# VectorE makes a block product's residual one step later in a three-layer kernel bound by TensorE

## The chip, the cores and the metric

The kernel runs on one core of one Trainium2 chip. The metric is the device time of one execution in microseconds (us), lower is better. The core's engines are TensorE (PE; its weight loads are shown apart, as PEld), VectorE (DVE), ScalarE (ACT), GpSimd (POOL) and SyncE (SP, which issues the DMAs). They run side by side, each in its own order, and wait for one another by semaphores.

## The reference

Three layers follow each other; all numbers are float32.

```
# 1 attention: 2 batches, 8 heads, 768 tokens, head size 64; 8 global columns, a window of 96
a = softmax(scale * q @ k.T + bias, where kept);  x = (a @ v) as [1536, 512]
# 2 a dense mixture of 4 experts: w1 [4, 512, 1024], w2 [4, 1024, 512]
for e in range(4):
    h = np.maximum(x @ w1[e], 0.0)
    out += p[:, e:e + 1] * (h @ w2[e])
# 3 one more layer: 512 -> 1024, h * softmax(h), normalised, 1024 -> 512
```

The change concerns `np.maximum(x @ w1[e], 0.0)` in layer 2.

## The kernel before

A float32 matrix is held as a high part and a residual (value less high part), both in TensorE's `float32r` format, and a product is the sum of three matmuls: high by high, high by residual, residual by high. So each hidden value h is needed twice: as high part `hh`, which ScalarE writes as the relu of a PSUM bank, and as residual `hl`, which VectorE makes from the same bank and `hh`.

Layer 2 runs over eight half experts (`he` 0 to 7, half of w1's columns each). The 1536 tokens are three blocks of 512. From `he` 1 on, the first product x @ w1 of two blocks together is made by a scheme of Strassen's kind with seven block products in place of eight (`paired_groups`, lines 646 to 698). From `he` 2 on, the third block is done in the same way in two halves of 256 tokens (`tail_groups`, lines 567 to 608). Seven passes of the first and six of the second run in all, one pass of each in each `he`: first the tail, then its second product h @ w2 (four groups of twelve matmuls, `g2`, line 523), then the paired products, then eight groups `g2`.

In `paired_groups` the products come in the order 1, 2, 6, 5, 7, 4, 3, each for q = 0 and q = 1 in turn (below "7q0" is product 7 for q = 0). A product is six matmuls of 512 columns (line 676). The products of one q share three PSUM banks: 1, 6, 7 and 4 add up in bank a, 2 in bank b, 5 and 3 in bank c. After each product stands what reads it:

- After 1, 6 and 5 ScalarE copies the bank to SBUF (`kept`, line 681).
- After 2, 7 and 3 VectorE adds a kept copy and a bank into bank b or c ("the sum", line 684); then `hidden` (line 658) lets ScalarE write `hh` (the relu, line 662) and VectorE write `hl` ("the residual", line 663).
- After 4 there is no sum: `hidden` reads bank a itself.

`tail_groups` does the same for one q with twelve matmuls of 256 columns to a product (line 596), in the order 1, 2, 6, 5, 7, 3, 4; its copy, sum, relu and residual are lines 601, 606, 582 and 583.

Each engine works its instructions off in the order in which this code issues them; nothing reorders them. So the residual of a product stands on VectorE's queue directly behind its sum, and waits there for ScalarE's relu. Between the products `st.tick` (line 414) issues other work: weights are loaded and split on ScalarE and GpSimd, and pieces of the third layer's weights are converted from 64 bits with up to four VectorE instructions at a time (lines 186 to 203).

What waits for what around the change:

```
684  nc.vector.tensor_tensor(out=t, in0=kept[...], in1=ps, op=ALU.add)                # the sum
662  nc.scalar.activation(th, src, AF.Relu)                                           # hh
663  nc.vector.scalar_tensor_tensor(out=tl, in0=src, ..., in1=th, max, subtract)      # hl
529  if given and c0 == 2 * HALF and dt == 0:
530      terms.sort(key=lambda x: (x[2] is hl, x[0] % 2))
```

Product 4 adds on in bank a, which the sum after 7 reads, so 4q1 can start only when the sum after 7q1 is done. After a tail pass the first group `g2` takes all `hh` terms first and the `hl` terms last (line 530); its first matmul needs the relus after 2 and 3, since each of its operands holds columns of both.

Of the kernel before, what the change touches and what calls it, by code (L numbers as in the profile page):

```python
# [8 lines left out]
F32 = mybir.dt.float32  # L9
# [5 lines left out]
AF = mybir.ActivationFunctionType  # L15
ALU = mybir.AluOpType
# [35 lines left out]
def kernel(ctx, tc, ep, qk, vp, nn, pr, wall, w64, gl, out):  # L52
    nc = tc.nc
# [57 lines left out]
    with tc.manual_schedule():  # L111
# [27 lines left out]
        def iota(cols, step, base, cm):  # L139
# [23 lines left out]
                                       op0=ALU.is_le, op1=ALU.mult)  # L163
        nc.vector.scalar_tensor_tensor(out=fi, in0=ng, scalar=float(NG_MAX), in1=flg[:, 1:2],
                                       op0=ALU.is_le, op1=ALU.mult)
# [41 lines left out]
    def stream(arm):  # L207
# [148 lines left out]
        def refresh(he):  # L356

            def due(k, *ops):
                for f in ops:
                    st.due.setdefault(st.now + k, []).append(f)  # L360

            (load0, sums0, (r0, r1, s0, s1)), (load2, sums2, (r2, r3, s2, s3)) = (
                first_weights(8 * he + q) for q in (0, 2))
            load0()
            yield
            load2()
            if he == 1:
                due(2, r0[0], r1[0])
                due(3, r0[1], r1[1])
                due(4, r2[0], r3[0])  # L370
                due(5, r2[1], r3[1])
                due(7, sums0)
                due(8, s0[0], s1[0])
                due(9, s0[1], s1[1])
                due(10, sums2)
                due(12, s2[0], s3[0])
                due(13, s2[1], s3[1])
                return
            r0[0]()
            r1[0]()  # L380
            due(1, r0[1], r1[1], r2[0], r3[0])
            due(2, sums0)
            due(3, r2[1], r3[1], s0[0], s1[0])
            due(4, s0[1], s1[1])
            due(5, sums2)
            due(6, s2[0], s3[0])
            due(7, s2[1], s3[1])
# [88 lines left out]
        def two_tiles():  # L476
            return [st.hp.tile([128, 2, HALF], F32R, tag=tag, name=f"{arm}{tag}") for tag in ("hh", "hl")]
# [83 lines left out]
        def left(he, q, i):  # L561
            n = 8 * he + 2 * q
            w, k0 = {1: (st.pieces[n], 0), 2: (st.pieces[n], 2), 4: (st.pieces[n + 1], 2), 6: (st.pieces["S", n], 0),
                     3: (st.pieces["S", n], 2), 7: (st.pieces["S", n + 1], 0), 5: (st.pieces["S", n + 1], 2)}[i]
            return w.rearrange("p w (k f) -> p w k f", k=4)[:, :, k0:k0 + 2]

        def tail_groups(he, h3):

            q_ = HALF // 2
            lo, hi = slice(2 * HALF, 2 * HALF + q_), slice(2 * HALF + q_, 3 * HALF)  # L570
            right = {i: [[x[:, k0 + j, cols] for j in range(2)] for x in (xh, xl)]
                     for i, k0, cols in ((1, 0, lo), (2, 2, lo), (3, 2, hi), (4, 0, hi))}
            for i, f in ((5, 0), (6, 1), (7, 2)):
                right[i] = [[st.xt3[f][j][:, b] for j in range(2)] for b in range(2)]
            twos = [two_tiles() for _ in range(2)]
            for d, w in zip(h3, range(2)):
                d[:] = [twos[odd][w].rearrange("p h (q c) -> p q h c", q=2)[:, q] for q in range(2) for odd in range(2)]
            banks, kept = {}, {}

            def hidden(src, odd, half):  # L580
                th, tl = (x[:, half] for x in twos[odd])
                nc.scalar.activation(th, src, AF.Relu)  # L582
                nc.vector.scalar_tensor_tensor(out=tl, in0=src, scalar=0.0, in1=th.bitcast(F32),
                                               op0=ALU.max, op1=ALU.subtract)

            for i in (1, 2, 6, 5, 7, 3, 4):
                c = {1: "a", 6: "a", 7: "a", 4: "a", 2: "b", 5: "c", 3: "c"}[i]
                opens = i in (1, 2, 5)
                if opens:
                    banks[c] = st.psp.tile([128, 512], F32, tag="g", name=f"{arm}g")  # L590
                ps, x = banks[c], right[i]
                for q in range(2):
                    w = left(he, q, i)
                    for j in range(2):
                        for m, (a, b) in enumerate(((0, 0), (0, 1), (1, 0))):
                            nc.tensor.matmul(ps[:, q_ * q:q_ * q + q_], lhsT=w[:, a, j], rhs=x[b][j],  # L596
                                             start=(opens and q == j == m == 0), stop=(j == 1 and m == 2),
                                             skip_group_check=True)
                if i in (1, 6, 5):
                    kept[i] = sc_b[2 if i == 6 else 0]  # L600
                    nc.scalar.copy(kept[i], ps)
                elif i == 4:
                    hidden(ps, 1, 0)
                else:
                    t = banks["c" if i == 3 else "b"]
                    nc.vector.tensor_tensor(out=t, in0=kept[{2: 1, 7: 5, 3: 6}[i]], in1=ps, op=ALU.add)  # L606
                    hidden(t, i == 7, i != 2)
                yield i
# [37 lines left out]
        def paired_groups(he, h1, h2):  # L646

            lo, hi = slice(0, HALF), slice(HALF, 2 * HALF)

            def raw_x(k0, cols):  # L650
                return [[x[:, k0 + j, cols] for j in range(2)] for x in (xh, xl)]

            right = {1: raw_x(0, lo), 2: raw_x(2, lo), 3: raw_x(2, hi), 4: raw_x(0, hi)}
            for i, f in ((5, 0), (6, 1), (7, 2)):
                right[i] = [[xt[:, f, b, j] for j in range(2)] for b in range(2)]
            banks, kept, twos = {}, {}, []

            def hidden(src, dst, ft):
                if ft < 2:
                    twos[:] = two_tiles()  # L660
                th, tl = (x[:, ft // 2] for x in twos)
                nc.scalar.activation(th, src, AF.Relu)  # L662
                nc.vector.scalar_tensor_tensor(out=tl, in0=src, scalar=0.0, in1=th.bitcast(F32),  # L663
                                               op0=ALU.max, op1=ALU.subtract)
                dst[0][ft], dst[1][ft] = th, tl

            def product(q, i):
                c = {1: "a", 6: "a", 7: "a", 4: "a", 2: "b", 5: "c", 3: "c"}[i]
                if i in (1, 2, 5):
                    pool = st.ps1 if (q, i) == (1, 5) else st.psp  # L670
                    banks[q, c] = pool.tile([128, 512], F32, tag="g", name=f"{arm}g")
                ps = banks[q, c]
                w, x = left(he, q, i), right[i]
                for j in range(2):
                    for m, (a, b) in enumerate(((0, 0), (0, 1), (1, 0))):
                        nc.tensor.matmul(ps, lhsT=w[:, a, j], rhs=x[b][j],  # L676
                                         start=(i in (1, 2, 5) and j == 0 and m == 0), stop=(j == 1 and m == 2),
                                         skip_group_check=(i not in (1, 2, 5)))
                if i in (1, 6, 5):
                    kept[q, i] = sc_b[(2 if i == 6 else 0) + q]  # L680
                    nc.scalar.copy(kept[q, i], ps)
                if i in (2, 7, 3):
                    t = banks[q, "c" if i == 3 else "b"]
                    nc.vector.tensor_tensor(out=t, in0=kept[q, {2: 1, 7: 5, 3: 6}[i]], in1=ps, op=ALU.add)  # L684
                    hidden(t, *((h1, 2 * q) if i == 2 else (h2, 2 * q + 1) if i == 7 else (h2, 2 * q)))
                elif i == 4:
                    hidden(ps, h1, 2 * q + 1)

            for i in (1, 2, 6, 5, 7, 4, 3):
                for q in range(2):  # L690
                    product(q, i)
                if i == 4:
                    weights = refresh(he + 1) if he < NHE - 1 else iter(())
                    next(weights, None)
                yield i
            next(weights, None)
            if he == NHE - 1:
                st.second += range(14)
# [226 lines left out]

    def fast_arm():
        st = stream("f")
        with ExitStack() as es:
            enter = es.enter_context
# [418 lines left out]

    def general_arm():
        st = stream("g")  # L1350
        for _ in st.load_p():
            pass
# [170 lines left out]
```

## Time and profile before

| | |
|---|---|
| median of 3 runs | 740.16 us (740.01 to 740.42) |
| the profiled execution's own time | 740.11 us |
| its span, first to last instruction | 738.2 us |
| granted TensorE clock, mean | 0.999 |
| PE busy | 725.0 us (98%), 3917 matmuls |
| PEld busy | 601.8 us (82%) |
| DVE busy | 473.0 us (64%) |
| ACT busy | 293.2 us (40%) |
| POOL busy | 260.7 us (35%) |

A matmul's row in the trace lasts longer than the step from its start to the next one's, because matmuls are pipelined; a row with x6 merges six of them. A row of the windows gives a stretch, its length, the busy time of PE, PEld, DVE, ACT and POOL (with the number of instructions), the granted clock, the DMA engines' busy share and GB/s. "Idle before" in square brackets is the time in which the engine did nothing ahead of the row, and what ended it.

### The profile page before, as it was taken

The numbers are of one execution on the slowest core, as the hardware profiler recorded it, in microseconds if no ns is written. First come the engines' busy times: TensorE is split into PE (matmuls) and PEld (weight loads), VectorE is DVE, ScalarE is ACT, GpSimd is POOL, SyncE is SP. The second block draws the span as 40 slices with busy tenths as digits, with TensorE's granted clock in tenths as the row PEclk, the third lists the DMA queues.
The fourth block names the chain that finished last, engine by engine and source line by source line (L and its number), as shares of the span: only waits on it lengthen the run. The fifth ranks groups of instructions, "written<-read, shape, count | busy, mean of one in ns | idle before, by whom it ended". The sixth has DMA issues, their size and how long they took to land.

```text
span 738.2 us, 11012 instructions
## 1 busy us (share of the span) xinstructions
PE 725.0 (98%) x3917; PEld 601.8 (82%) x3917; DVE 473.0 (64%) x1040; ACT 293.2 (40%) x668; POOL 260.7 (35%) x294
## 2 busy tenths in 40 slices
PE   8999999999999999999999999999999999999997
PEld 6688877888888888888888888888888888888886
DVE  6787868647694686568568567766843546655551
ACT  4777766432532334133243334323333223243252
POOL 5600044475683164208306424630744231000000
PEclk9999999999999999999999999999999999999999
DMA  8633421212242232223222222322100910222221
GB/s 252 169 94 100 113 84 44 86 43 72 73 135 91 60 101 85 72 87 108 78 72 85 86 72 94 107 72 82 48 28 29 366 62 12 60 77 75 64 73 49
DMA packets 49984, 65.69 MB, mean 89 GB/s; under 512 B 6656, under 2 KB 31488, under 8 KB 49920
## 3 DMA queue, kind: packets, MB, share of 16 engines
q1 hardware_dynamic: 49360, 64.47, 28.0%
q8 instruction: 33, 0.54, 0.3%
q10 hardware_dynamic: 560, 0.43, 0.2%
q14 instruction: 31, 0.25, 0.1%
HBM read 49.12 MB, written 11.56 MB: 82 GB/s over the span
## 4 chain that ended last, share of the span: by engine, by line
PE 85%; DVE 5%; ACT 4%; issue 3%; POOL 2%; DMA 0%; DVEq 0%; ACTq 0%; POOLq 0%
PE fg L532 35%; PE fg L676 14%; PE fo L904 9%; PE fh L843 9%; PE fg L596 6%; PE fg L503 4%; PE x L1102 2%; PE sps L998 2%; PE pt L1080 2%; DVE fg L684 1%; DVE fg L606 1%; ACT fhh L582 1%; PE wp L1185 1%; ACT fhh L662 1%; DVE fhl L663 1%
## 5 line engine op out<-in xcount | busy, mean ns | idle before, releaser
L532 PE MATMUL fg<-fhh,wV 128*128 128x512 f32 (+1 forms) x800 | 243.5, 384 | 3.4 <-ACT fhh L582 3.3
L532 PEld LDWEIGHTS fg<-fhh,wV 128*128 128x128 f32 x800 | 148.3, 188 | 36.7 <-ACT fhh L582 4.5
L532 PE MATMUL fg<-fhl,wV 128*128 128x512 f32 (+1 forms) x400 | 149.3, 381 | 0.0
L532 PEld LDWEIGHTS fg<-fhl,wV 128*128 128x128 f32 x400 | 75.0, 188 | 14.7 <-DVE fhl L518 0.2
L303 POOL TENSOR_TENSOR wR<-kr,wR 128x512 fp32r<-128x512 f32 (+1 forms) x28 | 29.0, 1061 | 111.5 <-ACT wR L295 71.5
L663 DVE SCALAR_TENSOR_TENSOR fhl<-fg,fhh 128x512 fp32r<-128x512 f32 x56 | 38.1, 690 | 31.8 <-ACT fhh L662 31.8
L676 PE MATMUL fg<-xt,fwS 128*128 128x512 f32 x252 | 58.3, 389 | 0.0
L676 PE MATMUL fg<-xh,wR 128*128 128x512 f32 x168 | 56.0, 394 | 0.7
L662 ACT ACTIVATE fhh<-fg 128x512 fp32r<-128x512 f32 x56 | 32.7, 598 | 58.9 <-DVE fg L684 55.1
L676 PEld LDWEIGHTS fg<-xt,fwS 128*128 128x128 f32 x252 | 47.3, 188 | 9.8
L545 POOL TENSOR_TENSOR scr<-scr,kr 128x512 f32<-128x512 f32 x24 | 31.0, 1291 | 63.1 <-DVE kr L544 63.1
L904 PE MATMUL fo<-xt,ft 128*128 128x512 f32 (+1 forms) x234 | 51.8, 374 | 0.0
L540 DVE TENSOR_TENSOR fg<-fg,pb 128x512 f32<-128x512 f32 x60 | 41.6, 693 | 14.5 <-PE fg L532 14.4
L904 PEld LDWEIGHTS fo<-xt,ft 128*128 128x128 f32 x234 | 41.5, 188 | 7.6
L1058 ACT ACTIVATE p<-p,mn 128x256 f32<-128x256 f32 x68 | 33.8, 498 | 27.5 <-DVE mn L1053 27.5
L893 POOL TENSOR_SCALAR fva<-fva 128x1 f32<-128x1 f32 x12 | 3.2, 265 | 114.2 <-ACT scr L892 114.2
L541 DVE TENSOR_TENSOR scr<-fg,scr 128x512 f32<-128x512 f32 x60 | 41.5, 692 | 2.0
L684 DVE TENSOR_TENSOR fg<-kr,fg 128x512 f32<-128x512 f32 x42 | 28.9, 689 | 21.6 <-PE fg L676 18.8
L676 PEld LDWEIGHTS fg<-xh,wR 128*128 128x128 f32 x168 | 31.5, 188 | 10.0 <-DVE fg L684 3.6
L503 PE MATMUL fg<-xh,wR 128*128 128x512 f32 (+1 forms) x128 | 39.5, 373 | 0.0
L544 DVE TENSOR_TENSOR kr<-fg,pb 128x512 f32<-128x512 f32 x24 | 16.6, 692 | 31.4 <-PE fg L532 27.9
L200 ACT CAST fr<-fcvs 128x256 fp32r<-128x256 f32 x32 | 11.9, 373 | 61.1 <-DVE fcvs L196 48.4
(206 smaller groups left out, 1468.3 us busy)
## 6 DMA issues: line engine op xcount, KB each, us to landing
kr<-in_wall_dram SPq DMA_DIRECT2D x42, 256.0 KB, 2.7
fr<-in_w_dram SPq DMA_DIRECT2D x32, 256.0 KB, 2.6
w_dram<-fr SPq DMA_DIRECT2D x32, 256.0 KB, 2.4
v<-in_vp_dram SPq DMA_DIRECT2D x10, 512.0 KB, 3.5
frawt<-in_wall_dram SPq DMA_DIRECT2D x14, 256.0 KB, 2.7
xt<-w_dram SPq DMA_DIRECT2D x6, 512.0 KB, 9.9
kr<-in_qk_dram SPq DMA_DIRECT2D x22, 128.0 KB, 3.8
out_dram<-scr SPq DMA_DIRECT2D x11, 256.0 KB, 2.2
```

The source lines that it names most:

```text
L503: nc.tensor.matmul(ps[:, :n], lhsT=w[:, a, k], rhs=b[:, k, cols], start=(k == 0 and i == 0), stop=(k == 3 and i == 2))
L532: nc.tensor.matmul(ps[:, :n], lhsT=w[:, a, k], rhs=b[k], start=(i == 0), stop=(i == 11))
L540: nc.vector.tensor_tensor(out=ps[:, :n], in0=ps[:, :n], in1=pb[:, cols], op=ALU.mult)
L541: nc.vector.tensor_tensor(out=a, in0=ps[:, :n], in1=a, op=ALU.add)
L596: nc.tensor.matmul(ps[:, q_ * q:q_ * q + q_], lhsT=w[:, a, j], rhs=x[b][j], start=(opens and q == j == m == 0), stop=(j == 1 and m == 2), ...
L662: nc.scalar.activation(th, src, AF.Relu)
L663: nc.vector.scalar_tensor_tensor(out=tl, in0=src, scalar=0.0, in1=th.bitcast(F32), op0=ALU.max, op1=ALU.subtract)
L676: nc.tensor.matmul(ps, lhsT=w[:, a, j], rhs=x[b][j], start=(i in (1, 2, 5) and j == 0 and m == 0), stop=(j == 1 and m == 2), skip_group_ch ...
L684: nc.vector.tensor_tensor(out=t, in0=kept[q, {2: 1, 7: 5, 3: 6}[i]], in1=ps, op=ALU.add)
L843: nc.tensor.matmul(ps[:, hf], lhsT=a[:, k, cs], rhs=w[:, b], start=(k == 0 and i == 0), stop=(k == 3 and i == 2))
L904: nc.tensor.matmul(ps, lhsT=a[:, fc % 4], rhs=wo[fc][:, b, c0:c0 + n], start=(fc == 0 and i == 0), stop=(fc == 7 and i == 2))
L1058: nc.scalar.activation(p[:, a], p[:, a], AF.Exp, bias=mn[:, a:a + 1], scale=-1.0, accum_out=st_rs[u][:, a, 0:1])
```

## The change

A helper `rectified` keeps a list of residuals that have not been issued yet. It first issues those on the list, then the relu of the new product, and then puts the new product's residual on the list. Since the sum of a product is issued before `hidden` is called, the order on VectorE becomes: sum of this product, residual of the product before. The list is also emptied after a copy to `kept`, after product 4 in the tail and after product 3q1 in the paired products.

```
+        def rectified(residuals, src, th, tl):
+            while residuals:
+                residuals.pop(0)()
+            nc.scalar.activation(th, src, AF.Relu)
+            residuals.append(lambda: nc.vector.scalar_tensor_tensor(
+                out=tl, in0=src, scalar=0.0, in1=th.bitcast(F32), op0=ALU.max, op1=ALU.subtract))
...
             def hidden(src, odd, half):
                 th, tl = (x[:, half] for x in twos[odd])
-                nc.scalar.activation(th, src, AF.Relu)
-                nc.vector.scalar_tensor_tensor(out=tl, in0=src, scalar=0.0, in1=th.bitcast(F32),
-                                               op0=ALU.max, op1=ALU.subtract)
+                rectified(residuals, src, th, tl)
...
                     nc.scalar.copy(kept[i], ps)
+                    while residuals:
+                        residuals.pop(0)()
                 elif i == 4:
                     hidden(ps, 1, 0)
+                    residuals.pop(0)()
...
             def hidden(src, dst, ft):
                 if ft < 2:
                     twos[:] = two_tiles()
                 th, tl = (x[:, ft // 2] for x in twos)
-                nc.scalar.activation(th, src, AF.Relu)
-                nc.vector.scalar_tensor_tensor(out=tl, in0=src, scalar=0.0, in1=th.bitcast(F32),
-                                               op0=ALU.max, op1=ALU.subtract)
+                rectified(residuals, src, th, tl)
...
                     nc.scalar.copy(kept[q, i], ps)
+                    while residuals:
+                        residuals.pop(0)()
...
+                if i == 3:
+                    residuals.pop(0)()
                 yield i
```

VectorE's order in the paired products of `he` 4, from the sum after 7q0 on. Before (lines 684 and 663 are sum and residual; the number behind `fg` is the bank that is read; 193 to 198 are a conversion of weights):

```order
L684 TENSOR_TENSOR fg_3790<-kr_78,fg_3768 128x512
L663 SCALAR_TENSOR_TENSOR fhl_3857<-fg_3790,fhh_3856 128x512
L684 TENSOR_TENSOR fg_3802<-kr_78,fg_3776 128x512
L663 SCALAR_TENSOR_TENSOR fhl_3857<-fg_3802,fhh_3856 128x512
L663 SCALAR_TENSOR_TENSOR fhl_3876<-fg_3768,fhh_3875 128x512
L663 SCALAR_TENSOR_TENSOR fhl_3876<-fg_3776,fhh_3875 128x512
L193 TENSOR_SCALAR fcvs_1830<-fr64_3767 128x256
L194 SCALAR_TENSOR_TENSOR fcvs_1830<-fr64_3767,fcvs_1830 128x256
L198 TENSOR_TENSOR fr64_3767<-fr64_3767,fcvs_1830 128x256
L684 TENSOR_TENSOR fg_3827<-kr_78,fg_3827 128x512
L663 SCALAR_TENSOR_TENSOR fhl_3903<-fg_3827,fhh_3902 128x512
L684 TENSOR_TENSOR fg_3835<-kr_78,fg_3835 128x512
```

The same place with the change (sum is now line 692, residual line 571):

```order
L692 TENSOR_TENSOR fg_3790<-kr_78,fg_3768 128x512
L692 TENSOR_TENSOR fg_3801<-kr_78,fg_3776 128x512
L571 SCALAR_TENSOR_TENSOR fhl_3857<-fg_3790,fhh_3856 128x512
L571 SCALAR_TENSOR_TENSOR fhl_3857<-fg_3801,fhh_3856 128x512
L571 SCALAR_TENSOR_TENSOR fhl_3875<-fg_3768,fhh_3874 128x512
L193 TENSOR_SCALAR fcvs_1830<-fr64_3767 128x256
L194 SCALAR_TENSOR_TENSOR fcvs_1830<-fr64_3767,fcvs_1830 128x256
L198 TENSOR_TENSOR fr64_3767<-fr64_3767,fcvs_1830 128x256
L692 TENSOR_TENSOR fg_3827<-kr_78,fg_3827 128x512
L571 SCALAR_TENSOR_TENSOR fhl_3875<-fg_3776,fhh_3874 128x512
L692 TENSOR_TENSOR fg_3835<-kr_78,fg_3835 128x512
```

The sum after 7q1 has moved ahead of the residual of 7q0, and the residual of 4q1 has moved behind the conversion and the sum after 3q0.

VectorE's order in the tail pass of `he` 4, from the sum after 2 to the last residual. Before (sum line 606, residual line 583):

```order
L606 TENSOR_TENSOR fg_3595<-kr_78,fg_3595 128x512
L583 SCALAR_TENSOR_TENSOR fhl_3578<-fg_3595,fhh_3577 128x512
L606 TENSOR_TENSOR fg_3595<-kr_78,fg_3581 128x512
L583 SCALAR_TENSOR_TENSOR fhl_3580<-fg_3595,fhh_3579 128x512
L606 TENSOR_TENSOR fg_3626<-kr_78,fg_3626 128x512
L583 SCALAR_TENSOR_TENSOR fhl_3578<-fg_3626,fhh_3577 128x512
L583 SCALAR_TENSOR_TENSOR fhl_3580<-fg_3581,fhh_3579 128x512
```

With the change (sum line 614, residual line 571):

```order
L614 TENSOR_TENSOR fg_3595<-kr_78,fg_3595 128x512
L571 SCALAR_TENSOR_TENSOR fhl_3578<-fg_3595,fhh_3577 128x512
L614 TENSOR_TENSOR fg_3595<-kr_78,fg_3581 128x512
L614 TENSOR_TENSOR fg_3626<-kr_78,fg_3626 128x512
L571 SCALAR_TENSOR_TENSOR fhl_3580<-fg_3595,fhh_3579 128x512
L571 SCALAR_TENSOR_TENSOR fhl_3578<-fg_3626,fhh_3577 128x512
L571 SCALAR_TENSOR_TENSOR fhl_3580<-fg_3581,fhh_3579 128x512
```

Here the sum after 3 has moved ahead of the residual of 7; the rest stands as it stood. On PE, ACT, POOL and SP no instruction moves.

## Rows read from the trace of the kernel before

**Rows 1.** The page: busy time, share of the span, instructions.
```profile
PE 725.0 (98%) x3917; PEld 601.8 (82%) x3917; DVE 473.0 (64%) x1040; ACT 293.2 (40%) x668; POOL 260.7 (35%) x294
```

**Rows 2.** Waits: who waited for whom, us in total, times, longest.
```profile
PEld fg L676 <- DVE fg L684: 3.6, 7, 0.5
...
PE fg L532 <- ACT fhh L582: 3.3, 6, 0.6
```

**Rows 3.** The chain that ended last, 329 to 430 us: start, us, what.
```profile
346.58 7.21 PE fg L596 x60
...
387.86 21.76 PE fg L532 x96
```

**Rows 4.** Windows: one pass of a half expert, `he` 4: us, busy by engine.
```profile
368.42:431.45 63.03, 62.38 (x314) 52.85 (x313) 44.57 (x85) 22.15 (x43) 25.22 (x24) 1.00 0.26 81
```

**Rows 5.** Timeline of DVE and ACT, paired products of `he` 4, 380 to 388 us.
```profile
380.77 0.70 DVE L684 TENSOR_TENSOR fg<-kr,fg 128x512 f32<-128x512 f32 x1 [1.98 <-PE fg L676]
381.50 0.60 ACT L662 ACTIVATE fhh<-fg 128x512 fp32r<-128x512 f32 x1 [1.57 <-DVE fg L684]
382.13 0.69 DVE L663 SCALAR_TENSOR_TENSOR fhl<-fg,fhh 128x512 fp32r<-128x512 f32 x1 [0.66 <-ACT fhh L662]
382.74 0.69 DVE L684 TENSOR_TENSOR fg<-kr,fg 128x512 f32<-128x512 f32 x1
386.41 0.42 DVE L193 TENSOR_SCALAR fcvs<-fr 128x256 int32<-128x256 int32 x1
```

**Rows 6.** Timeline of PE and PEld, same place, 381 to 390 us.
```profile
381.86 0.39 PE L676 MATMUL fg<-xh,wR 128*128 128x512 f32 x1
382.77 0.19 PEld L676 LDWEIGHTS fg<-xh,wR 128*128 128x128 f32 x1
382.99 0.98 PE L676 MATMUL fg<-xh,wR 128*128 128x512 f32 x2
383.48 0.19 PEld L676 LDWEIGHTS fg<-xh,wR 128*128 128x128 f32 x1 [0.52 <-DVE fg L684]
383.81 0.39 PE L676 MATMUL fg<-xl,wR 128*128 128x512 f32 x1
387.69 0.39 PE L532 MATMUL fg<-fhh,wV 128*128 128x512 f32 x1
389.96 0.39 PE L532 MATMUL fg<-fhl,wV 128*128 128x512 f32 x1
```

**Rows 7.** Timeline of the tail pass of `he` 4, 353 to 360 us.
```profile
353.61 0.28 PE L596 MATMUL fg<-xh,fwS 128*128 128x256 f32 x1
353.87 0.70 DVE L606 TENSOR_TENSOR fg<-kr,fg 128x512 f32<-128x512 f32 x1 [2.22 <-PE fg L596]
355.05 0.28 PE L596 MATMUL fg<-xh,wR 128*128 128x256 f32 x1
355.23 0.69 DVE L583 SCALAR_TENSOR_TENSOR fhl<-fg,fhh 128x512 fp32r<-128x512 f32 x1 [0.66 <-ACT fhh L582]
355.84 0.69 DVE L606 TENSOR_TENSOR fg<-kr,fg 128x512 f32<-128x512 f32 x1
356.37 0.28 PE L596 MATMUL fg<-xh,wR 128*128 128x256 f32 x1
356.56 1.09 ACT L582 ACTIVATE fhh<-fg 128x512 fp32r<-128x512 f32 x2 [1.36 <-DVE fg L606]
357.20 2.14 PE L532 MATMUL fg<-fhh,wV 128*128 128x512 f32 x8 [0.55 <-ACT fhh L582]
359.18 1.08 PE L532 MATMUL fg<-fhl,wV 128*128 128x512 f32 x4
```

**Rows 8.** Groups by line: busy, mean ns, idle before: PE's rows of line 676.
```profile
L676 PE MATMUL fg<-xh,wR 128*128 128x512 f32 x168 | 56.0, 394 | 0.7
```

**Rows 9.** DVE's wait in a conversion; the load of a piece (KB, us to landing).
```profile
DVE fr L203 <- ACT fr L200: 3.0, 5, 1.0
...
fr<-in_w_dram SPq DMA_DIRECT2D x32, 256.0 KB, 2.6
```

More of the change, by code (lines that the diff above doesn't have):

```diff
@@ L577, in tail_groups @@
                 d[:] = [twos[odd][w].rearrange("p h (q c) -> p q h c", q=2)[:, q] for q in range(2) for odd in range(2)]
-            banks, kept = {}, {}
+            banks, kept, residuals = {}, {}, []
             def hidden(src, odd, half):
                 th, tl = (x[:, half] for x in twos[odd])
-                nc.scalar.activation(th, src, AF.Relu)
-                nc.vector.scalar_tensor_tensor(out=tl, in0=src, scalar=0.0, in1=th.bitcast(F32),
-                                               op0=ALU.max, op1=ALU.subtract)
+                rectified(residuals, src, th, tl)
             for i in (1, 2, 6, 5, 7, 3, 4):
@@ L655, in paired_groups @@
                 right[i] = [[xt[:, f, b, j] for j in range(2)] for b in range(2)]
-            banks, kept, twos = {}, {}, []
+            banks, kept, twos, residuals = {}, {}, [], []
             def hidden(src, dst, ft):
```

## The prediction

> **What bounds the kernel now.** The page's busy time first: PE is busy for 725.0 of 738.2 us, the next engine, DVE, for 473.0 [rows 1]. So only time in which TensorE stands still can be won, some 13 us by this count, and the reader should look for what stops it. The view of the waits names what the change can touch [rows 2]: 7 weight loads of the paired products waited 0.5 us each for the sum (line 684), and 6 first matmuls of `g2` after a tail pass waited 0.6 us each for a relu (line 582). 7 and 6 are the numbers of paired and of tail passes, so it is the same place each time, and I work out one pass, `he` 4.
>
> Pace without a stall: 96 matmuls of 512 columns in 21.76 us, 0.227 us a step, and 60 of 256 columns in 7.21 us, 0.120 us [rows 3]. A pass has 228 of the first and 84 of the second, which makes 51.7 + 10.1 = 61.8 us; it lasts 63.03 [rows 4]. TensorE thus loses 1.2 us in a pass. The timelines show where.
>
> *Paired products.* Product 4q0 starts at 381.86; its last weights are loaded at 382.77 for a matmul at 382.99 [rows 6]. One step later, 383.00, those of 4q1 would be loaded, for a matmul at 383.22. They are loaded at 383.48, after 0.52 us of waiting, and the matmul behind the first starts at 383.81 where 383.45 was due: 0.36 us late. By the first matmul of `g2`, 19 steps after 382.99, it is 387.69 for 387.30, 0.39 late. The load waited for the sum after 7q1 (382.74 to 383.43), and that sum, on VectorE's queue, for the residual of 7q0 at 382.13, which in turn stood 0.66 us idle until the relu of 7q0 (from 381.50) was there [rows 5].
>
> *Tail.* The last matmul of product 4 starts at 356.37; `g2` was due at 356.49. Its first relu runs from 356.56, and the load and matmul start at 357.20. The ninth matmul starts at 359.18, due at 356.49 + 8 x 0.227 = 358.31: 0.87 us late. The relu waited for the sum after 3 (355.84 to 356.53), and this one for the residual of 7 (from 355.23) [rows 7]. 0.39 + 0.87 = 1.26, the loss found above.
>
> **The change part by part.** No instruction is added or removed; VectorE does the same work in another order, and PE, ACT, POOL and SP keep theirs.
>
> *The sum after 7q1 ahead of the residual of 7q0.* The sum after 7q0 starts at 380.77; 7q0's last matmul started seven steps ahead of 381.86, at 380.27, so a sum starts 0.50 us after the start of the last matmul it needs [rows 5, 6]. 7q1's last started at 381.63, so its sum can run from 382.13 to 382.82; VectorE is free then (the sum before it ends at 381.47). From the sum's end to the load it was 383.43 to 383.48, so the load is released at 382.87, and it is due at 383.00. The stall goes, with 0.13 us to spare. Worth 0.36 to 0.39 us; I take 0.38, and for 7 passes **2.7 us**.
>
> *The sum after 3 ahead of the residual of 7 in the tail.* The sum after 7 starts at 353.87; the last matmul of 7 started one step before 353.61, at 353.49, so the lag is 0.38 us. The last of product 3 started one step before 355.05, at 354.93: its sum can start at 355.31, where it was 355.84, and VectorE is free from 354.57. All behind it comes 0.53 us earlier: relu at 356.03, `g2` released at 356.67 [rows 7]. That is still 0.18 us after the due 356.49, so the relu of 3 is late next, and some 0.35 us of the 0.87 stays. The relu of 4 is needed by the fifth matmul; product 4's last matmul plus 0.38 is 356.75, its relu ends by 357.35, and the fifth matmul's load is due about 357.5. It costs nothing. Worth 0.53 us; bounds are 0.35 (if something takes a third of it back) and 0.71 (the whole distance from 356.49 to 357.20). For 6 passes **3.2 us**, 2.1 to 4.3.
>
> *Sums after 2q1 and 3q1 moved forward.* No matmul waits for them in any row of the waits, so they are worth 0. They let ScalarE's relus and VectorE's later work start earlier, under cover of the products that follow.
>
> *Residuals moved back.* The residual of 4q1 now stands behind the conversion and the sum after 3q0. It is needed by the eleventh matmul of `g2` (389.96, 389.57 without the stall), whose load is due at 389.35 [rows 6]. VectorE: residuals of 7q0, 7q1 and 4q0 follow the relus and end about 384.9; then three or four conversion instructions of 0.42 us, 0.46 from start to start, end at 386.3 or 386.7 [rows 5]; the sum after 3q0 (its product's last matmul is at 385.73 by then, plus 0.50) ends by 387.4, the residual by 388.0. That leaves 1.3 us. In the tail the residuals of 7, 3 and 4 are needed from the ninth matmul on, about 358.6; they end near 356.6, 357.4 and 358.1. Cost 0 in both, as long as nothing holds VectorE longer than these margins. The bank of product 7q0 is freed later for `g2`, by about 383.5 for 387.3: 0.
>
> Sum: 2.7 + 3.2 = 5.9 us. The profiled execution took 740.11 us, 1.9 more than its span, and is 0.05 under the median; 740.16 - 5.9 = **734.3 us**. The bounds of the two terms, 2.5 + 2.1 and 2.7 + 4.3, make 733.2 to 735.6.
>
> One weighing. Matmul rows of line 676 show 0.7 us of idle time before them in all [rows 8], 0.1 a pass, though the start times show 0.36: the row after a stall is longer (0.98 for two; a row of 0.39 and one step of 0.227 make 0.62), and idle time is counted from its recorded start. The Trainium skill's page "Perfetto Trace Analysis" (Identifying the Most-Contended Engine) says matmul busy time is a poor measure, since matmuls are pipelined, and asks for weight-load time instead. By the matmul rows the paired term would be 0.7 and the sum 3.9 (736.3); by the loads' waits, 3.6 us in 7 [rows 2], it would be at most 3.6 and the sum 6.8 (733.4). I go by the start times, between the two.
>
> **The rivals.**
> - *The paired stall stays.* The load of 4q1 has only 0.13 us to spare; if the two sums cannot follow that closely, or the load waits for something else that ends at the same time, only the tail's 3.2 us comes: 737.0 us. For it: the narrow margin. Against: a later sum would still cut most of the 0.5. The same page (Optimization Strategy) warns that a gap that repeats can mean buffers have run out; then the order of the queue would be no cure. Against that, the row names the sum, and product 4 adds to the bank that 7 used, with no new buffer. Chance 0.06.
> - *Only the paired stall goes.* The tail's relu of 3 may be held by another wait of the sum after 3. Then 740.16 - 2.7 = 737.5. Against: no idle time but the residual lies between the two sums now. Chance 0.04.
> - *Nothing measurable changes*, because later waits give it back: 740 us. Against: from 387.86 on TensorE runs 96 matmuls without a piece in between [rows 3]. Chance 0.03.
> - *Slower.* The residual of 4q1 now queues behind the conversion. If that instruction must wait for its piece to land, VectorE stands, and `g2` waits for `hl`. A load takes 2.6 us to land [rows 9]; held for all of it from where the queue gets there, `g2` loses 2.6 - 1.3 = 1.3 us in each of 7 passes, 9.1 us, against 5.9 won: 743.4 us. It decides from 2.1 us of holding a pass on (1.3 of margin and 5.9 / 7). Against: the longest such wait of a conversion in the trace is 1.0 us, on ScalarE [rows 9]. Chance 0.03.
>
> **How the numbers follow.** The forecast, both stalls shortened as worked out, has 0.84. The range must reach beyond its own 733.2 to 735.6 by the first rival, and a little below for what earlier sums might free besides: 733.0 to 737.0. A measurement of this kernel tells about 0.2%, 1.5 us. Faster by more: forecast and the first two rivals, 0.84 + 0.06 + 0.04, less a little for what none of them names: 0.93. Within 0.2%: 0.04. Slower: 0.03.
>
> **What would show it.** In the profile after, no weight load of the paired products waits for a sum; the two sums after 7q0 and 7q1 start 1.36 us apart, and a pass of `he` 4 takes about 62.1 us for 63.03. Before `g2` after a tail the wait for the relu falls from 0.55 us to under 0.1 and the sum after 3 starts 0.38 us after its product's last matmul. The prediction is wrong if a wait of a matmul for a residual shows up, or if the passes do not shorten by 0.9 us each.

## The result and the profile after

| | before | with the change |
|---|---|---|
| median | 740.09 us, 4 runs (739.93 to 740.42) | 734.20 us, 4 runs (734.00 to 734.41) |
| ratio | | 0.992, 95% interval 0.9903 to 0.9937 |
| the profiled execution's own time and span | 740.11 and 738.2 us | 734.20 and 732.3 us |
| one pass of a half expert | 63.03 us | 62.10 us |

The kernel is 5.9 us faster, 0.8%; 734.3 had been forecast. Both profiled executions reach the first paired product at the same time (179.15 us before, 179.13 now), so the whole of the gain lies behind it, in the passes.

The page, busy time by engine, of the kernel with the change:

```profile
PE 722.8 (99%) x3917; PEld 602.2 (82%) x3917; DVE 473.0 (65%) x1040; ACT 295.2 (40%) x668; POOL 260.7 (36%) x294
```

VectorE does the same 473.0 us of work in as many instructions [rows 1]. Matmul busy time fell by 2.2 us where the execution took 5.9 us less: a stalled matmul's row is drawn longer, so part of what was won had been counted as busy. The Trainium skill's page "Perfetto Trace Analysis" (Identifying the Most-Contended Engine) warns of this measure, and here the trace agrees; but the weight loads' busy time, which it takes as a share of the span instead, does not size the gain either: it stays (601.8 and 602.2 us) while the span gets shorter. Start times do.

Windows of two passes, each from the first paired product of one half expert to that of the next (us, then busy time of PE, PEld, DVE, ACT and POOL):

```profile
365.58:427.68 62.10, 62.05 (x314) 52.93 (x313) 44.75 (x85) 22.40 (x43) 25.23 (x24) 1.00 0.26 82
427.68:489.78 62.10, 62.05 (x314) 52.94 (x313) 44.23 (x84) 22.83 (x45) 25.18 (x24) 1.00 0.27 90
```

Each takes 0.93 us less than 63.03 [rows 4]. The starts in the chain divide it: from the first paired product to its `g2` it was 387.86 - 368.42 = 19.44 us [rows 3, 4] and is 384.62 - 365.58 = 19.04 (the chain is shown below), 0.40 less; from there to the next paired product, with the tail, it was 431.45 - 387.86 = 43.59 and is 427.68 - 384.62 = 43.06, 0.53 less. Waits (in total, times, longest):

```profile
PEld fg L532 <- ACT fhh L570: 1.5, 6, 0.3
...
DVE fhl L571 <- ACT fhh L570: 4.9, 7, 0.9
```

Lines 570 and 571 are now relu and residual of both passes, 692 the paired sum, 614 the tail's. Of [rows 2], the seven waits of paired loads for a sum are gone without a successor, and so are the matmuls' six waits for the tail's relu; the loads still wait for that relu, 0.25 us each. No row has a matmul or a load waiting for a residual of line 571.

The chain that ended last, from the tail to the next one:

```profile
353.02 0.71 DVE fg L614
...
353.75 0.60 ACT fhh L570
...
354.40 11.18 PE fg L532 x48
365.58 19.04 PE fg L682 x84
384.62 21.76 PE fg L532 x96
```

The 84 paired matmuls now run in one piece of 19.04 us, 0.227 us a step, with no sum between them. In the tail the chain still passes through the sum after 3 and its relu, in front of `g2`.

The paired products of half expert 4, timeline of VectorE, to be set beside [rows 5]:

```profile
377.93 0.70 DVE L692 TENSOR_TENSOR fg<-kr,fg 128x512 f32<-128x512 f32 x1 [2.58 <-PE fg L682]
379.29 0.70 DVE L692 TENSOR_TENSOR fg<-kr,fg 128x512 f32<-128x512 f32 x1 [0.66 <-ACT fhh L570]
379.90 2.04 DVE L571 SCALAR_TENSOR_TENSOR fhl<-fg,fhh 128x512 fp32r<-128x512 f32 x3
...
383.91 0.68 DVE L571 SCALAR_TENSOR_TENSOR fhl<-fg,fhh 128x512 fp32r<-128x512 f32 x1
```

of the matmuls of 7q1 and the first of 4q0:

```profile
377.66 1.52 PE L682 MATMUL fg<-xt,fwS 128*128 128x512 f32 x6
379.02 0.39 PE L682 MATMUL fg<-xh,wR 128*128 128x512 f32 x1
```

and of the weight loads at the same place:

```profile
379.93 0.41 PEld L682 LDWEIGHTS fg<-xh,wR 128*128 128x128 f32 x2
...
386.50 0.19 PEld L532 LDWEIGHTS fg<-fhl,wV 128*128 128x128 f32 x1
```

The sums after 7q0 and 7q1 start 1.36 us apart, which is six steps of 0.227, and the three residuals follow in a row with no wait of 0.1 us or more. The row of the second sum names a relu, that of 7q0, because it ends just before; but the sum starts 0.50 us after the start of its product's last matmul (379.02 - 0.23 = 378.79), and the sum after 7q0, which has no relu ahead of it, keeps the same distance (377.66 - 0.23 = 377.43). So it waits for its matmuls now. The second load of the row at 379.93 is the first of 4q1: it came 0.22 us behind the load before it, as every load does, some 0.1 us after the sum's end (379.29 + 0.70) had released it. The residual of 4q1 ends at 383.91 + 0.68 = 384.59; the load that needs it is at 386.50. That is a margin of 1.9 us.

The tail of half expert 4, timeline, to be set beside [rows 7]:

```profile
352.63 0.28 PE L601 MATMUL fg<-xh,fwS 128*128 128x256 f32 x1
...
353.02 0.70 DVE L614 TENSOR_TENSOR fg<-kr,fg 128x512 f32<-128x512 f32 x1 [0.76 <-PE fg L601]
...
353.75 1.23 ACT L570 ACTIVATE fhh<-fg 128x512 fp32r<-128x512 f32 x2 [0.86 <-DVE fg L614]
...
354.07 0.28 PE L601 MATMUL fg<-xh,wR 128*128 128x256 f32 x1
354.40 1.68 PEld L532 LDWEIGHTS fg<-fhh,wV 128*128 128x128 f32 x8 [0.26 <-ACT fhh L570]
354.40 2.11 PE L532 MATMUL fg<-fhh,wV 128*128 128x512 f32 x8
...
356.36 1.07 PE L532 MATMUL fg<-fhl,wV 128*128 128x512 f32 x4
```

The sum after 3 starts 0.39 us behind the start of its product's last matmul (352.63). Its relu ends 353.75 + 0.60, and `g2` starts at 354.40 where 354.07 + 0.12 = 354.19 was due. The ninth matmul of `g2` starts at 356.36 for 354.19 + 8 x 0.227 = 356.00: of the 0.87 us, 0.36 is left, and the matmul's own row shows no idle time for it.

### The profile page after: what moved, and what is told of

Same layout as the page of the kernel before. It is cut to its first block, busy times and chain, and to the rows that moved or that the text cites. A ratio compares the mean times of both kernels' runs of the same rounds, so it can differ in the third digit from the quotient of the medians.

```text
span 732.3 us, 11023 instructions
## 1 busy us (share of the span) xinstructions
PE 722.8 (99%) x3917; PEld 602.2 (82%) x3917; DVE 473.0 (65%) x1040; ACT 295.2 (40%) x668; POOL 260.7 (36%) x294
## 4 chain that ended last, share of the span: by engine, by line
PE 94%; DVE 3%; ACT 2%; issue 1%; DMA 0%; DVEq 0%; ACTq 0%
PE fg L532 36%; PE fg L682 18%; PE fo L914 9%; PE fh L853 9%; PE fg L601 7%; PE fg L503 5%; PE x L1112 2%; PE sps L1008 2%; PE pt L1090 2%; PE wp L1195 1%; DVE fg L614 1%; DVE p L1050 1%; PE fpt L894 1%; ACT p L1068 1%; PE g L1131 0%
## 5 line engine op out<-in xcount | busy, mean ns | idle before, releaser
L570 ACT ACTIVATE fhh<-fg 128x512 fp32r<-128x512 f32 x80 | 47.5, 598 | 65.5 <-DVE fg L692 39.1
L571 DVE SCALAR_TENSOR_TENSOR fhl<-fg,fhh 128x512 fp32r<-128x512 f32 x80 | 54.1, 687 | 6.8 <-ACT fhh L570 4.9
L540 DVE TENSOR_TENSOR fg<-fg,pb 128x512 f32<-128x512 f32 x60 | 41.6, 694 | 23.7 <-PE fg L532 23.5
L682 PE MATMUL fg<-xh,wR 128*128 128x512 f32 x168 | 54.0, 389 | 0.0
L687 ACT COPY kr<-fg 128x512 f32<-128x512 f32 x42 | 24.5, 589 | 32.5 <-PE fg L682 32.5
```

Of the source, the lines that this page charges most:

```text
L540: nc.vector.tensor_tensor(out=ps[:, :n], in0=ps[:, :n], in1=pb[:, cols], op=ALU.mult)
L571: residuals.append(lambda: nc.vector.scalar_tensor_tensor(out=tl, in0=src, scalar=0.0, in1=th.bitcast(F32), op0=ALU.max, op1=ALU.subtract))
L682: nc.tensor.matmul(ps, lhsT=w[:, a, j], rhs=x[b][j], start=(i in (1, 2, 5) and j == 0 and m == 0), stop=(j == 1 and m == 2), skip_group_ch ...
```

## The experiments

Diffs are against the kernel with the change. The theory is the prediction's: two places, two sums that stood behind a residual which waited for ScalarE. The rivals are that only one of the two counts, that the other moves give something, and that the residual moved back is close to costing time.

### Each half of the change alone

The tail gets the old order back (`e1_paired_only`):

```
             def hidden(src, odd, half):
                 th, tl = (x[:, half] for x in twos[odd])
                 rectified(residuals, src, th, tl)
+                while residuals:
+                    residuals.pop(0)()
...
                     hidden(ps, 1, 0)
-                    residuals.pop(0)()
```

> The new order only in the paired products; in the tail every residual stands behind its own sum again. Theory (two separate stalls of TensorE, each worth what its timeline shows): the 7 paired stalls go, the 6 tail stalls stay as before: 740.1 - 7 x 0.39 = 737.4 us; weight loads of the paired products wait for no sum, the first matmul after each tail waits 0.55 us again; a pass of he 4 takes 62.6 us. Rival (the gain is one thing, such as VectorE being less loaded as a whole): the time lies near 734 or near 740, not between.

Measured: 737.53 us (737.36 to 737.61), ratio 0.9964 (0.995 to 0.9977) to 740.13 of the kernel before. The tail's waits are back and no paired load waits for a sum; a pass takes 62.60 us, 0.43 less than before. Waits:

```profile
PEld fg L532 <- ACT fhh L570: 4.6, 6, 0.8
...
PE fg L532 <- ACT fhh L570: 3.3, 6, 0.6
```

The other way round (`e2_tail_only`), the paired products get the old order back:

```
                 th, tl = (x[:, ft // 2] for x in twos)
                 rectified(residuals, src, th, tl)
+                while residuals:
+                    residuals.pop(0)()
...
-                if i == 3:
-                    residuals.pop(0)()
                 yield i
```

> The new order only in the tail; in the paired products every residual stands behind its own sum again. Theory: 740.1 - 6 x 0.53 = 736.9 us, the 7 loads of 4q1 wait 0.5 us for the sum again, a pass of he 4 takes 62.5 us. Together with the run that changes the paired products alone, the gains add up to that of the whole change (5.9 us). Rival (the second stall hides behind the first, or one repair opens the other's wait): the two gains do not add up.

Measured: 737.65 us (737.24 to 738.09), ratio 0.9966 (0.9952 to 0.998), 0.75 us above what was expected. Waits:

```profile
PEld fg L684 <- DVE fg L694: 3.6, 7, 0.5
...
PEld fg L532 <- ACT fhh L570: 1.5, 6, 0.3
```

The paired wait is that of [rows 2] to the tenth, the tail's is that of the change. Its passes are 62.53 to 62.55 us, 0.48 less than before. Most of the miss lies ahead of them: in this profile the first paired product starts at 179.60 us, 0.45 later than in the one of before, though nothing that runs earlier was edited; the rest is 0.05 us in each of 6 passes. In the medians the halves bring 2.6 and 2.5 us, 5.1 of the 5.9 (the other profile, too, starts its passes 0.19 us late). By passes they add up: 0.43 + 0.48 = 0.91 of the 0.93 that the change brings.

### Only one residual moved in the paired products

`e3_seven_only` keeps the tail as changed, and of the paired moves only the one of 7q0's residual behind the sum after 7q1:

```
                 elif i == 4:
                     hidden(ps, h1, 2 * q + 1)
+                while residuals and (q, i) != (0, 7):
+                    residuals.pop(0)()
...
-                if i == 3:
-                    residuals.pop(0)()
```

> The tail as changed; in the paired products only the residual of 7q0 is moved behind the next sum, and the residuals of 2q0, 2q1, 7q1, 4q0, 4q1, 3q0 and 3q1 stand behind their own relus as before. Theory (only the sum after 7q1 is waited for by TensorE): the same as the whole change, 734.2 us, within 0.3. Rival (the earlier sums after 2q1 and 3q1 bring part of the gain): slower than the whole change by up to 2.7 us, 737.

Measured: 734.33 us (734.09 to 734.74), ratio 0.9921 (0.9907 to 0.9934), the time of the change. And this although VectorE waits for relus in front of residuals for 28.4 us, where with the change it is 4.9:

```profile
DVE fhl L571 <- ACT fhh L570: 28.4, 41, 1.8
```

So the other 23.5 us that VectorE waits less in front of residuals with the whole change are worth nothing. One move in the paired products and one in the tail make the whole gain.

### How far the moved residual is from costing time

The residual of 4q1 is written several times over, three times in `e4_two_more` and six times in `e5_five_more`, which holds VectorE at the place of the fourth rival. The values are the same. For the first:

```
                 elif i == 4:
                     hidden(ps, h1, 2 * q + 1)
+                    if q:
+                        residuals.extend(residuals[-1:] * 2)
```

> The change, with the residual of 4q1 made three times in place of once (the same values into the same place), so that it is finished about 1.3 us later. Theory (VectorE may hold that residual for 1.3 to 1.9 us before TensorE notices, by the profile after: it ends at 384.6, its load is due at 386.5): no loss, 734.2 us, within 0.5. Rival (the residual already stands at the edge, and anything behind it costs): about 7 x 1.3 = 9 us more.

Measured: 734.61 us (734.11 to 734.98), ratio 0.9923 (0.9908 to 0.9938). One load in the whole execution waited for a residual, in the first pass:

```profile
PEld fg L532 <- DVE fhl L571: 0.4, 1, 0.4
```

With `* 5` in place of `* 2`:

> The change, with the residual of 4q1 made six times, so that it is finished 3.1 to 3.6 us later. Theory: past the margin of 1.3 to 1.9 us TensorE waits for the residual, 1.2 to 2.1 us in each of 7 passes: 742 to 748 us, slower than the kernel before, with a wait of the second product's loads for line 571 on VectorE. Rival (TensorE has other slack, or the first product's residuals are not needed that early): under 737 us.

Measured: 748.12 us (747.26 to 748.89), ratio 1.0104 (1.0089 to 1.0119), now slower than before. Waits:

```profile
PEld fg L532 <- DVE fhl L571: 13.9, 7, 2.6
...
PE fg L532 <- DVE fhl L571: 11.0, 7, 2.2
```

and the chain at that place in half expert 4:

```profile
390.98 0.70 DVE fg L692
391.68 0.60 DVE fhl L571
...
392.30 0.70 DVE fhl L571
...
395.20 0.70 DVE fhl L571
...
395.95 4.15 PE fg L532 x17
```

A repetition takes 0.72 us (five from 391.58, where the timeline has the first residual's start, to 395.20), so five hold the residual back by 3.6 us. In half expert 4 the load that waited went at 395.94, 1.80 us late by its row, which leaves 3.6 - 1.8 = 1.8 us of cover, close to the 1.9 read off above. The passes, from one first paired product to the next, agree: three take 63.81 or 63.82 us, 1.7 more than with the change, and two 64.07, 2.0 more, so that 1.9 and 1.6 us are covered; the `g2` of the last, which has no next one, loses as much as in the three.

The first pass is another matter: 66.18 us, 4.1 more, which is more than the hold. Its load waited for 2.6 us, the longest in the rows above, so only some 1.0 is covered there; `e4_two_more` says the same (two repetitions, 1.44, less the wait of 0.43). The rest is TensorE's clock. Windows of that pass (the granted clock is the third figure from the end):

```profile
195.00:202.50 7.50, 5.50 (x25) 4.22 (x23) 6.40 (x11) 2.29 (x5) 4.15 (x6) 1.00 0.32 106
...
203.50:205.50 2.00, 2.00 (x6) 1.52 (x6) 1.93 (x4) 1.99 (x5) 1.27 (x2) 0.50 0.62 179
...
206.50:210.00 3.50, 3.50 (x17) 2.88 (x16) 3.33 (x8) 0.00 (x0) 3.19 (x5) 1.00 0.38 133
```

TensorE had stood for 2.2 us (the longest wait of a matmul above) until 202.68. With that the clock fell to 0.50, which is 1.2 GHz instead of 2.4, for 3.4 us, in which a step took 0.43 us instead of 0.227. That makes some 1.5 us of the 4.1. The other six passes kept 1.00. It seems not to happen in every execution: two of the four have a mean granted clock of 0.997 (748.77, the one profiled, and 748.89 us), two of 0.999 (747.26 and 747.47).

The rival's mechanism is real. With 1.9 us covered in four passes, 1.6 in two and 1.0 in one, and the clock left aside, a hold of about (5.9 + 11.8) / 7 = 2.5 us in each pass would undo the gain; this is an estimate from these covers.

### What the tail has left: the relu in two halves

After the change `g2` waits in each tail for the relu of 3. Its first load needs only the first half of the columns. `e6_relu_halves` writes that relu in two instructions of 256 columns:

```
-            nc.scalar.activation(th, src, AF.Relu)
+            for cols in [slice(0, 512)] if not halved else [slice(0, 256), slice(256, 512)]:
+                nc.scalar.activation(th[:, cols], src[:, cols], AF.Relu)
...
-                rectified(residuals, src, th, tl)
+                rectified(residuals, src, th, tl, half and not odd)
```

> The change, and in the tail the relu after product 3 is made in two instructions of 256 columns, the half that the first matmul of the second product reads first. Theory (what is left of the tail's stall, 0.36 us in the profile after, hangs on the end of that relu): the first half ends some 0.23 us sooner than the whole one, so 6 x 0.23 = 1.4 us less: 732.8 us, unless the relu after 4, one fixed cost later on ScalarE, becomes the wait. Rival (the first load after a tail waits for something else that ends at the same time): 734.2 us or more.

Measured: 733.25 us (733.00 to 733.64), ratio 0.9908 (0.9893 to 0.9923). Three passes by windows:

```profile
303.00:364.88 61.88, 61.88 (x313) 52.94 (x313) 43.29 (x82) 21.39 (x41) 25.14 (x24) 1.00 0.31 92
364.88:427.12 62.24, 62.05 (x313) 52.94 (x313) 44.73 (x85) 22.36 (x44) 25.25 (x24) 1.00 0.27 82
427.12:489.00 61.88, 61.88 (x313) 52.94 (x313) 44.22 (x84) 22.87 (x46) 25.21 (x24) 1.00 0.30 91
```

A pass is 0.22 us shorter, but for one. That one contains the tail of half expert 5; the chain there:

```profile
414.37 0.40 issue
414.77 0.71 DVE fg L615
415.48 0.02 issue
415.50 0.40 ACT fhh L571
...
415.94 11.18 PE fg L532 x48
```

Where the change has 0.04 us of "issue" ahead of the sum, this pass has 0.40: VectorE stood for 0.36 us that no row explains. In the other tails the loads of `g2` show no wait, as in half expert 4, timeline:

```profile
353.27 0.39 ACT L571 ACTIVATE fhh<-fg 128x256 fp32r<-128x256 f32 x1 [0.85 <-DVE fg L615]
...
353.47 0.19 PEld L602 LDWEIGHTS fg<-xh,wR 128*128 128x128 f32 x1
353.59 0.28 PE L602 MATMUL fg<-xh,wR 128*128 128x256 f32 x1
353.70 1.68 PEld L532 LDWEIGHTS fg<-fhh,wV 128*128 128x128 f32 x8
353.71 2.10 PE L532 MATMUL fg<-fhh,wV 128*128 128x512 f32 x8
355.42 0.87 PEld L532 LDWEIGHTS fg<-fhl,wV 128*128 128x128 f32 x4
355.65 1.07 PE L532 MATMUL fg<-fhl,wV 128*128 128x512 f32 x4
```

The ninth matmul is at 355.65 for 353.71 + 8 x 0.227 = 355.52, so 0.13 us are still lost. To ask whether that is the relu of 4, `e7_both_halves` halves it as well (`half != odd` in place of `half and not odd`):

> The change, and in the tail the relus after products 3 and 4 are each made in two instructions of 256 columns. With the relu after 3 alone in halves, 0.13 us of the tail's stall was left in a clean pass, where the fifth matmul waits for the relu after 4. Theory (that relu is what is late next): 6 x 0.1 = 0.6 us less than there, 6 x 0.33 = 2.0 us less than the change: 732.3 us. Rival (one more fixed cost on ScalarE delays the residuals): 733.2 us or more.

Measured: 733.10 us (732.97 to 733.34), ratio 0.9905 (0.989 to 0.992). Passes are 61.89 to 61.91 us, again with one of 62.23 at the same place, and the ninth matmul is still 0.14 late. So it is not the relu of 4. The trace points at the relu of 3 once more: in the timeline above its first half ends at 353.27 + 0.39 = 353.66, and the first load of `g2` starts at 353.70, where 353.47 + 0.12 = 353.59 was due. That is 0.11 of the 0.13 us, and no idle time is shown for it. In every tail of the change and of both halved versions this load starts 0.05 us after the end of the relu or its first half, in half expert 5 too, where the relu itself comes later. No run moves that half any further, so this is read off and not tested. What holds the 0.36 us of half expert 5 stays open.

The change itself, run again beside `e7_both_halves` on the same chip (`e8_change_again`; `e6_relu_halves` ran on another, where `e3_seven_only` gave 734.33 us too):

> The change itself once more, beside the runs with halved relus on the same chip: 734.2 us, within 0.4.

Measured: 734.33 us (734.15 to 734.52), ratio 0.9921 (0.9907 to 0.9934). Every run of both halved versions was faster than every run of the change; at 1.1 and 1.2 us, under 0.2%, the difference is less than I had said a measurement can tell, but the passes show it too: from the first paired product to that of the last pass the halved versions take 0.9 us less. The two versions themselves, 733.25 and 733.10 us, can't be told apart.

## Why the prediction was right

- *Where TensorE stood still.* Two places in a pass, 0.39 and 0.87 us. Right: each half of the change removes its own wait and leaves the other's as it was (`e1_paired_only`, `e2_tail_only`).
- *The paired term*, 0.38 us in 7 passes, 2.7. From the first paired product to its `g2` a pass is 0.40 us shorter, so 2.8: right. The margin of 0.13 us at the load was the prediction's narrowest point, and it held: some 0.1 us. The rival that the stall stays fell.
- *The tail term*, 0.53 us in 6 passes, 3.2. The rest of a pass is 0.53 us shorter, so 3.2: right. "The relu of 3 is late next" and "some 0.35 us stays" were right too: the six load waits are for that relu and 0.36 us stayed; halving the relu gives 0.22 of it back, not all. The prediction of the wait had been under 0.1 us; the matmuls show none, the loads 0.26.
- *Sum.* 2.8 + 3.2 = 6.0 us, for 5.9 measured. The halves alone show 0.43 and 0.48 us a pass in place of 0.40 and 0.53: a few hundredths of a us lie in the other stretch of the pass, and no run shows why. The term for all the other paired moves was 0, and `e3_seven_only` bears that out.
- *Start times, not rows.* Taken from the matmuls' idle time the paired term was 0.7 us, from the loads' waits 3.6; by start times it is 2.8. The two end values would have missed by 2.1 us down and by 0.8 up.
- *Residuals moved back cost 0.* Right. The margin was put at 1.3 us; it is 1.9 in four passes, 1.6 in two and about 1.0 in the first, where 1.3 was too much. The point of 2.1 us, from which the fourth rival decides, is some 2.5. After the change no residual made a load or a matmul wait, so no conversion came near it. What the rival left out is the clock, which fell in one stop of `e5_five_more` and made that pass 1.5 us longer still.
- *The rule of the repeating gap* (the Trainium skill, "Perfetto Trace Analysis", Optimization Strategy) did not apply: no buffer was added, and the gaps went with the order of a queue.

What was wrong were expectations. `e2_tail_only` came out 0.75 us high, mostly because a difference of some tenths ahead of the passes was left out of its range. `e5_five_more` ended just above its 742 to 748 us, since the clock was left out. `e6_relu_halves` gave 1.1 us for the 1.4 expected, as one of its tails gained nothing. And in `e7_both_halves` the 0.13 us left over was put down to the relu of 4, from which nothing came.

## What to carry to other kernels

On an engine that works in order, an instruction which waits for another engine also holds what stands behind it. Where what is behind feeds the busiest engine, and the waiting instruction does not, put the waiting one later and work out its new margin; here two moves in a pass were worth 0.9 us, and 23 us less of other waits on the same engine nothing. After such a move ask what is late next: an instruction of which only a part is needed first can be split, which is what the Trainium skill's page "Perfetto Trace Analysis" (Optimizing Scalar/DVE Operations) advises for an engine that isn't saturated and causes gaps on another, and here it gave 0.22 us a pass.

## What the runs showed of the hardware that was not expected

- Six repetitions of one residual, from the same inputs to the same place, follow each other at 0.72 us, each starting 0.03 us after the end of the one before. A residual followed by an unrelated sum takes 0.61 from start to start [rows 5].
- With a stop of TensorE of 2.2 us in the first pass of `e5_five_more` its granted clock fell from 1.00 to 0.50 for 3.4 us, and matmuls of 512 columns started 0.43 us apart.
- The first paired product starts between 179.03 and 179.66 us in ten profiles of kernels that are alike up to there. A difference of half a microsecond between two versions has to be looked for in the stretch that was edited.
- The 0.36 us of half expert 5 appear in both halved versions and not in the change, at the same sum, with no releaser in the trace.
